# RWKV time mixing ahead of a SwiGLU FFN: both halves of mixing's products issued together, random trials on the start's schedule, the input flag made earlier

The chip is a Trainium2, one of its cores is used. The metric is the time of one execution in device microseconds (us), median of the runs; lower is better. The profiler's span of the same execution is some 1.7 to 1.8 us shorter than its time. Engine names in the profiles: PE is TensorE (PEld its weight loads), DVE VectorE, ACT ScalarE, POOL GpSimd, SP SyncE.

## The reference

```python
def _attn_ref(r, k, v, w, u):                 # B, H, S, D = 4, 8, 768, 48
    state = np.zeros((B, H, D, D)); y = np.zeros_like(r)
    for t in range(S):
        kt, vt, rt = (k[:, :, t], v[:, :, t], r[:, :, t])
        cur = np.einsum('bhd,bhe->bhde', u[None] * kt, vt)
        y[:, :, t] = np.einsum('bhd,bhde->bhe', rt, state + cur)
        state = w[None, :, :, None] * state + np.einsum('bhd,bhe->bhde', kt, vt)
    return y

def _moe_ref(x, w_gate, w_val, w_out, rms_g): # x: 3072 tokens x 384; d_ff 1536
    xn = x / np.sqrt(np.mean(x * x, axis=-1, keepdims=True) + 1e-06) * rms_g
    g = xn @ w_gate
    return (g / (1 + np.exp(-g)) * (xn @ w_val)) @ w_out
```

All in float32. The weights can arrive as 64-bit words, which the kernel rounds itself.

## The kernel before

The sequence is cut into 12 chunks of 64 steps. For a chunk, time mixing has four kinds of TensorE product, each for two halves of the batch: scores (`products`, 32 matmuls a half), outputs (`outputs`, 48), states (`states`, 32), and the sum of squares for the norm. The FFN then takes the chunk's 256 tokens. Chunks 0 and 1 and the mixing of 2 and 3 are the start, in which the weights are also loaded and rounded; from chunk 2 on, five blocks take two chunks each (the body, and the last block without mixing).

The start is ordered on the host by a list schedule. Every piece of work has an engine, a planned cost, its inputs, and for loads a planned landing time; the pieces are then issued in the order of their planned starts, and each engine works strictly in that order:

```python
    def run(self, cells, first, free, idle=None):
        goals, t = {}, first
        for i in cells:
            goals[i] = t
            t += self.ops[i][1]
        self.start = self.schedule(goals, free)
        ...                                       # cut: fillers for PE's clock
        for i in sorted(range(len(self.ops)), key=lambda i: (self.start[i], i)):
            ...
            self.ops[i][3]()                      # issue
    ...
    def loads(s):                                 # cost on SyncE, landing behind it
        add("SP", 2.6 if s == 0 else 2.0, [], ["CHr0", "CHr1", "CHk0", "CHk1"], lambda: load_chan(s), land=2)
    ...
        for half in range(2):                     # mixing in the start
            bank, key = next_at()                 # one of two PSUM banks
            add("PE", 0.97, [f"CHk{half}", f"MEr{half}", f"MOr{half}"], [key],
                lambda bank=bank, half=half: products(bank, half, CH[:, 1], ME, MO), name=f"A {s}")
            ...
```

The order of the body is written out: small letters are the first half, capitals the second (a scores, d diagonals, m masked copy, y outputs, u states; R and K decay r and k, 1 to 3 the bonus, h the state's k, r and n the norm):

```python
            plan = {
                (0, 2): "R", (1, 1): "K", (1, 4): "1", (2, 0): "2", (2, 2): "3d", (3, 0): "h", (3, 2): "aDm",
                (4, 0): "H", (4, 2): "AM", (4, 4): "y", (5, 2): "Y", (5, 4): "q", (5, 5): "u",
            }
        ...                                       # cut: six groups of seven FFN products
        mix(n, "U"), mix(n + 1, "R12")
        project(s, 0, False), mix(n, "r"), mix(n + 1, "3K")
        project(s, 0, True), mix(n + 1, "ad"), mix(n, "n")
        ...
```

48 checks read the weights once more (a load into one buffer, two ScalarE passes): 40 in four of the blocks and two behind each of the last four projections. Their sum becomes a flag; every engine loads it into a register and branches over a general path if it is 0.

## Time and profile before

674.57 us (674.41 to 676.01 over three runs; the profiled one took 675.09). Cut where the FFN's products, the blocks and the projections begin in the trace:

| stage | us |
|---|---|
| first FFN product begins | 27.35 |
| from there to the first block | 134.20 |
| four blocks with mixing | 105.56 + 102.97 + 102.97 + 101.07 = 412.57 |
| last block, to TensorE's last product | 85.82 |
| from there to the end | 13.36 |

TensorE is busy 96% of 673.3 us and VectorE 58%. TensorE's own rows do not say whether it could be faster.

### The profile page before, as it was taken

The numbers are of one execution on the slowest core, as the hardware profiler recorded it, in microseconds if no ns is written. First come the engines' busy times: TensorE is split into PE (matmuls) and PEld (weight loads), VectorE is DVE, ScalarE is ACT, GpSimd is POOL, SyncE is SP. The second block draws the span as 40 slices with busy tenths as digits, with TensorE's granted clock in tenths as the row PEclk, the third lists the DMA queues.
The fourth block names the chain that finished last, engine by engine and source line by source line (L and its number), as shares of the span: only waits on it lengthen the run. The fifth ranks groups of instructions, "written<-read, shape, count | busy, mean of one in ns | idle before, by whom it ended". The sixth has DMA issues, their size and how long they took to land.

```text
span 673.3 us, 15350 instructions
## 1 busy us (share of the span) xinstructions
PE 649.6 (96%) x6546; PEld 507.8 (75%) x6546; DVE 388.0 (58%) x560; ACT 342.5 (51%) x952; POOL 44.4 (7%) x39
## 2 busy tenths in 40 slices
PE   9969999999999999999999999999999999999992
PEld 8957777877878766888766888766888866888651
DVE  6998987345875724676644666652676553455200
ACT  5678470764262474474573574672564573433222
POOL 3434431000000000000000000000000000000000
PEclk9979999999999999999999999999999999999996
DMA  8997531262003141306341405332315221212141
GB/s 293 305 235 212 188 90 24 44 160 65 2 1 95 42 118 25 96 22 153 86 99 32 107 19 148 91 74 62 91 34 142 67 47 25 57 41 57 48 111 53
DMA packets 20079, 61.61 MB, mean 92 GB/s; under 512 B 3073, under 2 KB 6273, under 8 KB 18817
## 3 DMA queue, kind: packets, MB, share of 16 engines
q1 hardware_dynamic: 19696, 60.44, 33.8%
q8 instruction: 53, 0.87, 0.6%
q14 instruction: 26, 0.20, 0.1%
q10 hardware_dynamic: 304, 0.10, 0.1%
HBM read 55.81 MB, written 4.72 MB: 90 GB/s over the span
## 4 chain that ended last, share of the span: by engine, by line
PE 82%; DVE 8%; ACT 6%; DMA 2%; issue 2%; SPq 0%; DVEq 0%; ACTq 0%
PE po L90 24%; PE b L90 15%; PE a L90 10%; PE c L90 10%; PE first_c L90 4%; PE first_b L90 4%; PE py L90 4%; PE first_a L90 3%; PE at L90 3%; PE pa L90 3%; ACT MO L90 2%; PE pu L90 2%; DVE bits L90 2%; ACT ME L90 1%; DVE TOK L90 1%
## 5 line engine op out<-in xcount | busy, mean ns | idle before, releaser
L90 PE MATMUL po<-wo,h 128*128 128x384 f32 x480 | 162.5, 491 | 0.0
L90 PEld LDWEIGHTS po<-wo,h 128*128 128x128 f32 x480 | 89.2, 190 | 57.4 <-issue 0.3
L90 DVE TENSOR_TENSOR gv<-b,m 128x512 f32<-128x512 f32 x90 | 62.1, 690 | 66.3 <-PE b L90 65.6
L90 ACT ACTIVATE gv<-gv 128x512 f32<-128x512 f32 (+1 forms) x60 | 31.0, 518 | 49.6 <-DVE gv L90 49.6
L90 DVE TENSOR_TENSOR gv<-c,gv 128x512 f32<-128x512 f32 x60 | 41.4, 690 | 16.9 <-PE c L90 15.8
L90 ACT ACTIVATE ME<-dmask,du 64x64 f32<-64x64 f32 x176 | 43.8, 329 | 13.4 <-DVE du L90 13.0
L90 PE MATMUL a<-xa,wa 64*128 64x256 f32 x360 | 45.0, 382 | 1.9 <-DVE h L90 1.9
L90 PE MATMUL b<-xa,wa 64*128 64x256 f32 x360 | 45.3, 384 | 0.6 <-DVE gv L90 0.6
L90 ACT ACTIVATE MO<-dmask,du 64x64 f32<-64x64 f32 x176 | 44.4, 334 | 0.4
L90 PE MATMUL b<-t,wb 64*128 64x256 f32 x360 | 44.4, 379 | 0.0
L90 PE MATMUL c<-xb,s 64*128 64x256 f32 x360 | 44.3, 378 | 0.0
L90 PE MATMUL b<-t,s 64*128 64x256 f32 x360 | 44.0, 377 | 0.3 <-DVE gv L90 0.3
L90 PE MATMUL a<-xb,wb 64*128 64x256 f32 x360 | 43.9, 376 | 0.0
L90 PE MATMUL c<-t,s 64*128 64x256 f32 x360 | 43.9, 376 | 0.0
L90 PEld LDWEIGHTS a<-xa,wa 64*128 64x128 f32 x360 | 33.8, 187 | 8.8 <-DVE h L90 4.1
L90 PEld LDWEIGHTS b<-t,s 64*128 64x128 f32 x360 | 34.8, 187 | 4.7 <-DVE gv L90 0.7
L90 PEld LDWEIGHTS a<-xb,wb 64*128 64x128 f32 x360 | 34.8, 187 | 4.0
L90 PEld LDWEIGHTS c<-t,s 64*128 64x128 f32 x360 | 34.8, 187 | 4.0
L90 PEld LDWEIGHTS b<-t,wb 64*128 64x128 f32 x360 | 34.4, 187 | 4.4 <-DVE gv L90 0.3
L90 PEld LDWEIGHTS b<-xa,wa 64*128 64x128 f32 x360 | 33.4, 187 | 5.7 <-DVE gv L90 1.5
L90 PEld LDWEIGHTS c<-xb,s 64*128 64x128 f32 x360 | 34.5, 187 | 4.0
L90 ACT ACTIVATE gv<-a 128x256 f32<-128x256 f32 x30 | 11.4, 381 | 48.7 <-PE a L90 48.6
(146 smaller groups left out, 1100.7 us busy)
## 6 DMA issues: line engine op xcount, KB each, us to landing
TOK<-in_tok_dram SPq DMA_DIRECT2D x12, 768.0 KB, 4.9
chan<-in_chan_dram SPq DMA_DIRECT2D x22, 384.0 KB, 6.5
VS<-in_vpad_dram SPq DMA_DIRECT2D x24, 336.0 KB, 4.9
raw<-in_wot_dram SPq DMA_DIRECT2D x8, 576.0 KB, 5.7
again<-in_wka_dram SPq DMA_DIRECT2D x16, 288.0 KB, 2.8
out_dram<-o SPq DMA_DIRECT2D x48, 96.0 KB, 2.2
again<-in_wkb_dram SPq DMA_DIRECT2D x16, 288.0 KB, 2.9
again<-in_wot_dram SPq DMA_DIRECT2D x16, 288.0 KB, 2.8
```

What stands on the lines that cost most here:

```text
L90: return lambda *args, **kwargs: self.tc.keep_in_program_order(give(*args, **kwargs))
```

## The change

The intent: fewer changes between the forms of matmul on TensorE, a better order in the start, w, r and k ahead of u in the load queues, and the flag off the end of the program. Its core:

```diff
-    def run(self, cells, first, free, idle=None):
+    def run(self, cells, first, free, idle=None, trials=3000):
...
+        rng, best = random.Random(2), None
+        for trial in range(trials):
+            new = dict(goals)
+            if trial and rng.random() < 0.5:
+                a, by = rng.randrange(len(cells)), rng.uniform(-15, 15)
+                for i in cells[a : a + 1 + int(rng.expovariate(1 / 6))]:
+                    new[i] += by
+            elif trial:
+                new[rng.randrange(len(self.ops))] = rng.uniform(0, t)
+            start = self.schedule(new, free)
+            end = max(...) + 0.3 * sum(start[i] for i in cells) / len(cells)
+            if best is None or end <= best[0]:
+                best, goals = (end, start), new
...
-        add("SP", 2.6 if s == 0 else 2.0, [], ["CHr0", ...], lambda: load_chan(s), land=2)
+        add("SP", 2.3 if s == 0 else 1.8, [], ["CHr0", ...], lambda: load_chan(s), land=1.6)
...                      # in the start, from chunk 1 on: both halves one piece
+            add("PE", 2.35, score_keys[0] + score_keys[1], [two[0][1], two[1][1]],
+                lambda: [scores(0), scores(1)], name=f"A {s}")
...
-                (0, 2): "R", ..., (3, 2): "aDm",
-                (4, 0): "H", (4, 2): "AM", (4, 4): "y", (5, 2): "Y", (5, 4): "q", (5, 5): "u",
+                (0, 2): "R", ..., (3, 2): "D",
+                (3, 5): "aAm", (4, 1): "M", (4, 2): "H", (4, 4): "yY", (5, 3): "q",
...
+        mix(n, "uU"), mix(n + 1, "R123")
+        project(s, 0, False), mix(n, "r"), mix(n + 1, "KdD")
+        project(s, 0, True), mix(n + 1, "aA"), mix(n, "n")
+        project(s, 1, False), mix(n + 1, "mMh")
+        project(s, 1, True), mix(n + 1, "yYH")
...                      # checks: 6 now in the first block, 13 in the last; the load a turn ahead
-            for j in range(4):
-                project(s, j, False), project(s, j, True), check(), check()
...
+    project(s, 0, False), project(s, 0, True)
     pc = at_bank("pc")
-    nc.tensor.matmul(pc[0:1, 0:1], wrong, ones[:, 0:1], start=True, stop=True)
+    pe.matmul(pc[0:1, 0:1], wrong, ones[:, 0:1], start=True, stop=True)
+    n_bad = nc.values_load(bad[0:1, 0:1], min_val=0, max_val=1 << 20)
+    for j in range(1, 4):
+        project(s, j, False), project(s, j, True)
```

Planned costs of VectorE and ScalarE pieces also rise by 0.03 each, and other load times fall a little.

More of the change, by code (lines that the diff above doesn't have):

```diff
@@ L27 @@
+import random
 from collections import deque
@@ L107, in add @@
         n = len(self.ops)
+        if engine in ("DVE", "ACT"):
+            cost += 0.03
         self.ops.append((engine, cost, deps, give, land, port, name))
@@ L164, in run @@
             t += self.ops[i][1]
-        self.start = self.schedule(goals, free)
+        rng, best = random.Random(2), None
[8 more added lines that the diff above has]
+            start = self.schedule(new, free)
+            end = max(start[i] + self.ops[i][1] for i in cells) + 0.3 * sum(start[i] for i in cells) / len(cells)
+            if best is None or end <= best[0]:
+                best, goals = (end, start), new
+        self.start = best[1]
         busy = free["PE"]
@@ L209, in fast @@
     utab = c_tile([P, HP, D], "utab")
-    for z in range(2):
-        src = bass.AP(tensor=u_row.tensor, offset=u_row.offset + z * HP * D, ap=[[0, 64], [1, HP * D]])
-        act.dma_start(out=utab[64 - 64 * z : 128 - 64 * z].rearrange("p h d -> p (h d)"), in_=src)
     eps = c_tile([P, 1], "eps")
@@ L313, in load_v, with load_u @@
         sp.dma_start(out=VS[0:64, 1], in_=vpad[s, 0:64])
+    def load_u():
+        for z in range(2):
+            src = bass.AP(tensor=u_row.tensor, offset=u_row.offset + z * HP * D, ap=[[0, 64], [1, HP * D]])
+            sp.dma_start(out=utab[64 - 64 * z : 128 - 64 * z].rearrange("p h d -> p (h d)"), in_=src)
     wa = [c_tile([P, NQ, CC, P], f"wa_{i}") for i in range(WQ)]
@@ L340, in piece @@
         hi, lower = words[:, :, 1], words[:, :, 0].bitcast(U32)
-        p.add("SP", 1.6 * share, [], [r], lambda: sp.dma_start(out=raw, in_=part), land=2, name=f"load {n}")
+        p.add("SP", 1.35 * share, [], [r], lambda: sp.dma_start(out=raw, in_=part), land=1.8, name=f"load {n}")
         p.add(
@@ L588, in next_at @@
         return at[i], f"at{i}"
-    add("SP", 0.0, [], ["w"], lambda: None, land=2.8)
+    add("SP", 0.0, [], ["w"], lambda: None, land=2.4)
     add("DVE", 2.4, ["w"], ["pw"], powers, name="powers")
@@ L605, in loads @@
     def loads(s):
-        add("SP", 2.6 if s == 0 else 2.0, [], ["CHr0", "CHr1", "CHk0", "CHk1"], lambda: load_chan(s), land=2)
-        add("SP", 2.0, [], ["TOKr", "TOKk"], lambda: load_tok(s), land=2)
-        add("SP", 1.8, [], ["VSv"], lambda: load_v(s), land=2)
+        add("SP", 2.3 if s == 0 else 1.8, [], ["CHr0", "CHr1", "CHk0", "CHk1"], lambda: load_chan(s), land=1.6)
+        add("SP", 1.8, [], ["TOKr", "TOKk"], lambda: load_tok(s), land=1.8)
+        add("SP", 1.6, [], ["VSv"], lambda: load_v(s), land=1.8)
+        if s == 0:
+            add("SP", 0.5, [], ["utab"], load_u, land=1.8)
     def mixing(s):
@@ L616, in mixing @@
                 add(
-                    "PE", 0.97, ["ku", "CHr0", "CHr1"], [f"first{half}"],
+                    "PE", 1.05, ["ku", "CHr0", "CHr1"], [f"first{half}"],
                     lambda half=half: products(gv["a"][:, half], half, ku, CH[:, 0], CH[:, 0]), name=f"E {s}",
@@ L621, in mixing @@
             add("DVE", 0.95, ["TOKk"], ["TOKr"], lambda: bonus_1(s), port=True, name=f"bonus1 {s}")
-            add("DVE", 0.95, [], ["TOKr"], lambda: bonus_2(s), port=True, name=f"bonus2 {s}")
+            add("DVE", 0.95, ["utab"], ["TOKr"], lambda: bonus_2(s), port=True, name=f"bonus2 {s}")
             add("DVE", 0.94, ["TOKr"], ["du"], lambda: bonus_3(s), name=f"bonus3 {s}")
@@ L628, in mixing, with scores @@
             add(
-                "DVE", 0.05 + 0.585 * n, ["up"] + keys("CHr"), keys("MEr", "MEt"),
+                "DVE", 0.12 + 0.55 * n, ["up"] + keys("CHr"), keys("MEr", "MEt"),
                 lambda part=part: decay_r(s, *part), port=True, name=f"R {s}",
             )
-            add("ACT", 0.1 + 0.47 * n, keys("MEt"), keys("MOr"), lambda part=part: copy_r(s, *part), name=f"Rc {s}")
+            add("ACT", 0.16 + 0.44 * n, keys("MEt"), keys("MOr"), lambda part=part: copy_r(s, *part), name=f"Rc {s}")
             add(
-                "DVE", 0.05 + 0.585 * n, ["down"], keys("CHk"), lambda part=part: decay_k(s, *part), port=True,
+                "DVE", 0.12 + 0.55 * n, ["down"], keys("CHk"), lambda part=part: decay_k(s, *part), port=True,
                 name=f"K {s}",
             )
-        for half in range(2):
-            bank, key = next_at()
-            add(
-                "PE", 0.97, [f"CHk{half}", f"MEr{half}", f"MOr{half}"], [key],
-                lambda bank=bank, half=half: products(bank, half, CH[:, 1], ME, MO), name=f"A {s}",
-            )
+        two = [next_at() for _ in range(2)]
+        def scores(half):
+            products(two[half][0], half, CH[:, 1], ME, MO)
+        score_keys = [[f"CHk{half}", f"MEr{half}", f"MOr{half}"] for half in range(2)]
+        if quick:
+            for half in range(2):
+                add("PE", 1.05, score_keys[half], [two[half][1]], lambda half=half: scores(half), name=f"A {s}")
+        else:
+            add(
+                "PE", 2.35, score_keys[0] + score_keys[1], [two[0][1], two[1][1]], lambda: [scores(0), scores(1)],
+                name=f"A {s}",
+            )
+        for half in range(2):
+            bank, key = two[half]
             for side in range(2):
@@ L655, in mixing @@
                 )
+        pair = [next_at() for _ in range(2)]
+        output_keys = [[f"{x}{half}" for x in ("VSs", "MEr", "MOr", "MEt", "MOt")] for half in range(2)]
+        if quick:
+            for half in range(2):
+                add(
+                    "PE", 1.55, ["VSv"] + output_keys[half], [pair[half][1]],
+                    lambda half=half: outputs(pair[half][0], half), name=f"Y {s}",
+                )
+        else:
+            add(
+                "PE", 3.25, ["VSv"] + output_keys[0] + output_keys[1], [pair[0][1], pair[1][1]],
+                lambda: [outputs(pair[half][0], half) for half in range(2)], name=f"Y {s}",
+            )
         for half in range(2):
-            bank, key = next_at()
+            bank, key = pair[half]
             add(
-                "PE", 1.5, ["VSv"] + [f"{x}{half}" for x in ("VSs", "MEr", "MOr", "MEt", "MOt")], [key],
-                lambda bank=bank, half=half: outputs(bank, half), name=f"Y {s}",
-            )
-            add("ACT", 0.5, [key], [f"sq{half}"], lambda bank=bank, half=half: keep_squares(bank, half, sq), name=f"sq {s}")
-            add("ACT", 0.88, [key], [f"yT{half}"], lambda bank=bank, half=half: keep_outputs(bank, half, yT), name=f"yT {s}")
+                "ACT", 0.5, [key], [f"sq{half}"], lambda bank=bank, half=half: keep_squares(bank, half, sq),
+                name=f"sq {s}",
+            )
+            add(
+                "ACT", 0.88, [key], [f"yT{half}"], lambda bank=bank, half=half: keep_outputs(bank, half, yT),
+                name=f"yT {s}",
+            )
         bank, key = next_at()
@@ L680, in mixing @@
             add("DVE", 0.95, ["TOKk", "wk"], [f"KH{z}"], lambda z=z: state_k(s, z), port=True, name=f"h {s}")
-        for half in range(2):
-            bank, key = next_at()
-            add(
-                "PE", 0.97, ["KH0", "KH1", "khd", "VSv", f"VSs{half}"], [key],
-                lambda bank=bank, half=half: states(bank, half), name=f"U {s}",
-            )
+        last = [next_at() for _ in range(2)]
+        add(
+            "PE", 1.9, ["KH0", "KH1", "khd", "VSv", "VSs0", "VSs1"], [last[0][1], last[1][1]],
+            lambda: [states(last[half][0], half) for half in range(2)], name=f"U {s}",
+        )
+        for half in range(2):
+            bank, key = last[half]
             add("ACT", 1.07, [key], [f"VSs{half}"], lambda bank=bank, half=half: keep_states(bank, half), name=f"E {s}")
@@ L785, in warm @@
             pe.matmul(gv["c"][:, 0, 0:P], ones, ones, start=True, stop=True)
-    p.run(cells, 25.0, {"PE": 1.5, "DVE": 1.5, "ACT": 4.5, "POOL": 6.5, "SP": 1.2}, warm)
+    p.run(cells, 25.0, {"PE": 1.5, "DVE": 1.5, "ACT": 3.0, "POOL": 6.3, "SP": 1.7}, warm)
     def at_bank(name):
@@ L856, in fast @@
     again = deque(enumerate(parts))
+    staged = []
     def check():
-        if not again:
-            return
-        n, (src, k) = again.popleft()
-        raw = late["mine"].tile([P, CHECK], I64, name=f"again_{n}", tag="again")
-        nc.sync.dma_start(out=raw, in_=src[:, k * CHECK : (k + 1) * CHECK])
-        hi = raw.bitcast(I32).rearrange("p (n z) -> p n z", z=2)[:, :, 1].bitcast(FP32)
-        mag = late["mine"].tile([P, CHECK], FP32, name=f"mag_{n}", tag="mag")
-        act.activation(mag, hi, AF.Abs)
-        act.activation(mag, mag, AF.Relu, scale=-(2.0**15), bias=1.0, accum_out=seen[:, n : n + 1])
+        if staged:
+            n, raw = staged.pop()
+            hi = raw.bitcast(I32).rearrange("p (n z) -> p n z", z=2)[:, :, 1].bitcast(FP32)
+            mag = late["mine"].tile([P, CHECK], FP32, name=f"mag_{n}", tag="mag")
+            act.activation(mag, hi, AF.Abs)
+            act.activation(mag, mag, AF.Relu, scale=-(2.0**15), bias=1.0, accum_out=seen[:, n : n + 1])
+        if again:
+            n, (src, k) = again.popleft()
+            raw = late["mine"].tile([P, CHECK], I64, name=f"again_{n}", tag="again")
+            sp.dma_start(out=raw, in_=src[:, k * CHECK : (k + 1) * CHECK])
+            staged.append((n, raw))
     def group(s, m):
@@ L949, in fast @@
             plan = {
-                (0, 2): "R", (1, 1): "K", (1, 4): "1", (2, 0): "2", (2, 2): "3d", (3, 0): "h", (3, 2): "aDm",
-                (4, 0): "H", (4, 2): "AM", (4, 4): "y", (5, 2): "Y", (5, 4): "q", (5, 5): "u",
+                (0, 2): "R", (1, 1): "K", (1, 4): "1", (2, 0): "2", (2, 2): "3d", (3, 0): "h", (3, 2): "D",
+                (3, 5): "aAm", (4, 1): "M", (4, 2): "H", (4, 4): "yY", (5, 3): "q",
             }
@@ L954, in fast @@
             plan = {}
+        look = {(m, k) for m in range(NN // 2) for k in (2, 5) if m != 2}
+        if first_block:
+            look = {(m, k) for m, k in look if k == 5 or m == 4}
+        elif n == NS:
+            look |= {(2, 2), (2, 5), (5, 6)}
         for m in range(NN // 2):
@@ L962, in fast @@
                     mix(n, plan[m, k])
-                if not first_block and k in (2, 5) and m != 2:
+                if (m, k) in look:
                     check()
         if n == NS:
-            for j in range(4):
-                project(s, j, False), project(s, j, True), check(), check()
             break
-        mix(n, "U"), mix(n + 1, "R12")
-        project(s, 0, False), mix(n, "r"), mix(n + 1, "3K")
-        project(s, 0, True), mix(n + 1, "ad"), mix(n, "n")
-        project(s, 1, False), mix(n + 1, "ADmh")
@@ L973, in fast @@
-        project(s, 1, True), mix(n + 1, "yMH")
-        project(s, 2, False), mix(n + 1, "Yq")
+        mix(n, "uU"), mix(n + 1, "R123")
[3 more added lines that the diff above has]
+        project(s, 1, True), mix(n + 1, "yYH")
+        project(s, 2, False), mix(n + 1, "q")
         project(s, 2, True), mix(n + 1, "r")
-        project(s, 3, False), mix(n + 1, "un")
-        project(s, 3, True), mix(n + 1, "U")
+        project(s, 3, False), mix(n + 1, "n")
@@ L978, in fast @@
+        project(s, 3, True), mix(n + 1, "uU")
         for x in (1, 2, 3, 4):
             token_sum(n, x)
-    assert not again
+    assert not again and not staged
     tiny = c_tile(list(seen.shape), "tiny")
     if wide:
-        nc.vector.tensor_single_scalar(out=tiny, in_=seen, scalar=0.0, op=ALU.is_gt)
+        dve.tensor_single_scalar(out=tiny, in_=seen, scalar=0.0, op=ALU.is_gt)
     else:
-        nc.vector.memset(tiny, 0.0)
-    nc.vector.tensor_reduce(out=count[:, 1:2], in_=tiny, op=ALU.add, axis=AX.X)
+        dve.memset(tiny, 0.0)
@@ L989, in fast @@
+    dve.tensor_reduce(out=count[:, 1:2], in_=tiny, op=ALU.add, axis=AX.X)
     wrong = c_tile([P, 1], "wrong")
-    nc.vector.scalar_tensor_tensor(
+    dve.scalar_tensor_tensor(
         out=wrong, in0=count[:, 1:2], scalar=float(HP), in1=count[:, 0:1], op0=ALU.add, op1=ALU.subtract
     )
+    project(s, 0, False), project(s, 0, True)
     pc = at_bank("pc")
-    nc.tensor.matmul(pc[0:1, 0:1], wrong, ones[:, 0:1], start=True, stop=True)
-    nc.vector.tensor_copy(bad, pc[0:1, 0:1])
+    pe.matmul(pc[0:1, 0:1], wrong, ones[:, 0:1], start=True, stop=True)
@@ L998, in general @@
+    dve.tensor_copy(bad, pc[0:1, 0:1])
+    n_bad = nc.values_load(bad[0:1, 0:1], min_val=0, max_val=1 << 20)
+    for j in range(1, 4):
+        project(s, j, False), project(s, j, True)
+    return n_bad
 @with_exitstack
@@ L1404, in program @@
     chan, tok, vpad, wka, wkb, wot, cols, u_row, chan_0 = fast_args
-    fast(tc, chan, tok, vpad, wka, wkb, wot, cols, u_row, chan_0, out, bad)
-    n_bad = nc.values_load(bad[0:1, 0:1], min_val=0, max_val=1 << 20)
+    n_bad = fast(tc, chan, tok, vpad, wka, wkb, wot, cols, u_row, chan_0, out, bad)
     with tc.If(n_bad > 0):
```

## The prediction

> **What bounds the kernel now.** First the page's slices (tenths busy in 40 slices of 16.8 us):
>
> ```profile
> PE   9969999999999999999999999999999999999992
> DVE  6998987345875724676644666652676553455200
> PEclk9979999999999999999999999999999999999996
> ```
>
> TensorE (PE) is full from the fourth slice to the last but one; there are two holes, in the third slice, with a lowered clock, and at the end. VectorE (DVE) is the fuller engine only in the first 64 us. Then the busy time by stretch, cut where the stages change (stretch, its length, busy PE, weight loads, DVE, ACT, POOL, clock, DMA share, GB/s):
>
> ```profile
> 27.35:64.40 37.05, 31.44 (x364) 25.75 (x364) 33.38 (x42) 28.93 (x70) 17.59 (x12) 0.91 0.89 257
> 370.15:473.05 102.90, 102.71 (x1053) 79.40 (x1053) 58.78 (x83) 56.45 (x164) 0.00 (x0) 1.00 0.33 82
> 574.12:659.95 85.83, 85.82 (x601) 66.87 (x600) 29.41 (x49) 29.92 (x77) 0.00 (x0) 1.00 0.24 65
> 660.00:673.30 13.30, 0.19 (x2) 0.09 (x2) 0.70 (x4) 2.36 (x7) 0.00 (x0) 0.57 0.17 44
> ```
>
> So there are four regimes: a start bound by the chain to the first weights and by DVE; a body (five blocks of two chunks) in which PE alone sets the time; the last block, PE alone without time mixing; and 13.3 us in which PE has nothing to do. In the body the question is what PE's time is made of. The chain of waits there is PE from end to end (start, length, group):
>
> ```profile
> 401.99 1.08 PE pa L90 x32
> 403.07 1.50 PE b L90 x12
> 404.56 1.29 PE a L90 x12
> ...
> 437.70 3.87 PE po L90 x12
> 441.57 1.08 PE pa L90 x32
> 442.65 4.07 PE po L90 x12
> ```
>
> A product of 12 matmuls takes 1.29, but 1.50 behind a visit to time mixing (pa, py, pu); 12 projection matmuls take 3.87, but 4.07 behind one. Each visit costs 0.2 beyond its own time. Where the same chain has both halves together:
>
> ```profile
> 145.06 2.89 PE at L90 x96
> 147.94 1.50 PE first_c L90 x12
> ```
>
> 96 outputs matmuls in one visit take 2.89, against 2 x 1.52 for two visits of 48 (the row py x48 of the same view): 0.15 less. In the start, the timeline has 64 score matmuls from 12.83 to 14.84, 2.01 against 2 x 1.08: again 0.15. So one visit less saves 0.15 + 0.21 = **0.36 us**.
>
> Third, the hole in the start (timeline, then chain):
>
> ```profile
> 34.98 1.46 PE L90 MATMUL first_c<-xb,wb 64*128 64x256 f32 x12
> 41.80 0.37 PE L90 MATMUL at<-ME,chan 48*64 48x64 f32 x1 [5.35 <-DVE chan L90]
> ```
>
> ```profile
> 41.80 3.75 PE at L90 x64
> ```
>
> PE waits 5.35 us for chunk 1's decayed k. Afterwards the same 64 matmuls take 3.68 to the next start instead of 2.01, and the next 12 product matmuls 2.41 instead of 1.29: 1.7 + 1.1 = 2.8 more. The hole costs about 8.1 in all.
>
> Fourth, the end (timeline):
>
> ```profile
> 661.68 0.54 SPq L864 DMA_DIRECT2D again<-in_wot_dram  x1
> 664.79 0.46 ACT L90 ACTIVATE mag<-again 128x288 f32<-128x288 f32 x1 [3.39 <-DMA again<-in_wot_dram]
> 665.85 0.19 DVE L985 TENSOR_SCALAR tiny<-seen 128x48 f32<-128x48 f32 x1 [35.27 <-ACT mag L90]
> 666.75 0.15 DVE L995 CAST bad<-pc 1x1 int32<-1x1 f32 x1 [0.28 <-PE pc L994]
> ```
>
> The last product ends at 659.95 and the last store is issued at 660.48 to 661.6. Then comes one more weight check behind a DMA wait, the sum of the flags, its matmul and cast (to 666.9). The trace then has five register loads of the flag (to 667.5), the branch over the general path, and semaphores to 673.3.
>
> **What the Trainium skill says.** "TensorEngine Tiling (Array Packing)", Key Properties, says that changing the tiling mode drains TensorE; mixing's 48x64 and the FFN's 64x128 and 128x128 matmuls are different modes, and the trace agrees with 0.1 before and 0.1 after each change. "TensorE: Matmul & The Clock Gate", Part 1, puts the return to half clock at an idle window of about 3.4 us; the 5.35 us wait with the doubled durations behind it agrees, at a granted clock of 0.91 over that stretch. "Runtime: NRT & Kernel Launch", Instruction fetch mechanics, says that a taken branch to a page outside the window stalls on a fetch; the trace has 4.48 us of branch on PE, and 3.6 us from SyncE's branch (667.48) to its next instruction (671.06), so it agrees. "DMA: Bandwidth & Descriptors" gives some 2 us of fixed cost to a transfer; the page's median for the output store is 2.2.
>
> **The change, part by part.**
>
> *Halves together.* In a full block the PE order has 12 mixing visits, each of scores (pa), outputs (py), states (pu), for two chunks and two halves. The new plan has aA, yY and uU, so 6. Blocks 2, 4 and 6 lose 6 visits, block 8 loses 5 (chunk 11, the last, has no states): 23 x 0.36 = 8.3. In the scheduled start, outputs 1, states 0, states 1, scores 2 and states 2 stand apart in the trace, and scores 1 and 3, outputs 2 and 3 and states 3 already together: 5 x 0.36 = 1.8. The matmuls themselves stay the same, so nothing else of PE's time goes. All of it lies on the path, since PE is the path.
>
> *Random trials.* 3000 trials of a hill climb on the order of the start; no instruction more or less on the chip. What it can win is the 8.1 of the hole and delays ahead of the first product at 27.35. There DVE has non-urgent instructions in the way: the 2.63 us product for KH holds the reciprocal back by about 1, two weight conversions hold the first xa back by about 1.3 (26.11, where its bank was filled by 24.8). The first projection (3.87 us) is also held out of the hole only because its three gating DVE products of 0.42 stand at 42.8 to 46, not at 37. Against it, DVE is busy 33.4 of 37 us there, so moving one thing forward moves another back, and the trials optimise modelled times, not the chip's. I choose half of the hole: **4.0**.
>
> *w, r, k first.* The two loads of u leave ScalarE's queue and go behind the first loads of SyncE. Their packets began at 4.93, when those of w (to 5.6) and r, k (to 5.6) were nearly through, and ScalarE waited until 6.45 anyway. I give this 0 on its own.
>
> *Checks and flag.* 48 checks as before, now with the load issued one turn ahead: ScalarE loses the 26.6 us of DMA waits (9.9 + 9.6 + 7.1 in the waits), none of them on the path. All 48 are done before the last projections; the flag is made behind the first of four (7.74 us each, half of the two-chunk output). There PE must wait for its own matmul, the cast and its register load: from 666.52 to the end of the load at 667.43 in the old tail, with a switch, **+1.0**. At the end, the copy and store stay (to 661.6 for a PE end of 659.95); then SyncE's branch, 3.6, gives 665.2, and from there 2.2 as before (671.06 to 673.3): PE end + 7.45 instead of + 13.35, **-5.9**. PE's branch, 4.5 after its end, and the store's landing, 2.2 after its issue, are both shorter than that.
>
> *New waits.* Both mixing banks are now taken at once, and four masked copies (4 x 0.73) fall between scores and outputs. In the block there are 6 steps of 1.3 = 7.8 us between them; the second two copies stand behind the addition that follows the third step, so they end near 3 x 1.3 + 0.7 + 2 x 0.73 = 6.1, a margin of 1.7. Between projections there are 7.8 us too. Diagonals take 4 x 2.0 us of ScalarE, now issued earlier. I allow 1.0 over all blocks.
>
> Sum: 674.6 - 8.3 - 1.8 - 4.0 + 1.0 - 5.9 + 1.0 = **656.6**.
>
> **Rivals.**
>
> *The start does not move, or gets worse.* For it: DVE's 33.4 of 37 us, a model without the clock's fall after a wait, and paired scores and outputs in the start, which are harder to place. Against: the filler (the projection) is there, and the new costs (0.03 more per DVE and ACT instruction, DMA times nearer to the measured ones) make the model truer. Then 660.6; with 3 us lost, 663.6. The other way, with the whole hole gone and the first product 2 us earlier, 650.5.
>
> *DVE or the two banks become the bound in the block.* For it: the masked copies and the state product are bunched into little more than one group of 7 products (9.1 us), in which DVE already has 5.0: (62.1 + 41.4)/30 for the additions of the page's rows and 0.69 + 2 x 0.42 for h. Against: DVE is busy 58.8 of 102.9 over the block and PE waits for it 0.2 there. If each of four blocks waited 1 us more, 660.
>
> *The end does not shorten.* For it: the branch is taken later than the flag is read, so its fetch still follows the last instruction; PE could also lose more than 1.0 at the flag. Against: the 7 us from 659.95 to 666.9 contain nothing that needs the last product. At worst half of the 4.9 remains: 659.
>
> **Range and chances.** The body's 8.3 and the end's 4.9 are nearly counted (together +-2); the start is the wide term (+-4). The 2% line is 661.1; it takes both a start without gain and another step short to stay above it. I give 0.83 to faster, 0.16 to within 2%, 0.01 to slower; range 651 to 662.
>
> **What would show it right or wrong.** Right: scores x64 near 2.0, outputs x96 near 2.9, states x64 near 1.55 in the chain; blocks of about 100.9 us instead of 102.9; PE busy falling by about 10; the hole before chunk 1's scores under 3 us and no clock below 1 behind it; first steady block from about 156 instead of 161.55; a stop of about 1 us on PE between the first and second projection; 7.5 us from PE's end to the end. Wrong: PE waits on DVE gv or h or on masked copies inside the blocks, a new hole before 64 us, or more than 9 us after PE's end.

## The result, and the profile after

663.36 us (662.33 to 665.46 over four runs), against 674.99 of the kernel before in the same rounds: a ratio of 0.983, 95% interval 0.980 to 0.986. So it is faster by 1.7%, beyond the noise but not clear of 2%, and outside the predicted range. (Ratios are the mean time of one kernel's runs over that of the other's of the same rounds, so not quite the ratio of the medians quoted.)

The stages, from the traces (spans, so their sum is 1.7 to 1.8 below the times):

| stage, us | before | predicted | after | difference |
|---|---|---|---|---|
| first FFN product begins | 27.35 | | 35.28 | +7.93 |
| from there to the first block | 134.20 | | 126.96 | -7.24 |
| first block begins | 161.55 | 155.75 | 162.24 | +0.69 |
| four blocks | 412.57 | 405.3 | 406.58 | -5.99 |
| last block | 85.82 | 86.8 | 86.94 | +1.12 |
| tail | 13.36 | 7.45 | 6.39 | -6.97 |

The sum of the differences is -11.15, the spans' 673.3 and 662.2 differ by 11.1. Predicted was -18.0. Of the 6.9 that are missing, the start accounts for 6.5 (+0.7 where -5.8 was expected), the blocks for 1.3 more, and the tail gives 1.0 back. One trace is one run, and this one lies 0.6 above the median: four kernels below have the same start (e4_flag_end to e7_read_late), and in their traces the body begins at 160.0 to 160.9. So the start's shortfall is 4.3 to 6.5 us.

The body did what was expected. The chain of waits of the kernel after, around its third block (start, length, group):

```profile
404.23 2.01 PE pa L91 x64
406.24 1.50 PE c L91 x12
...
414.21 2.89 PE py L91 x96
...
440.91 7.94 PE po L91 x24
...
467.84 1.57 PE pu L91 x64
```

64 scores in 2.01, 96 outputs in 2.89, 64 states in 1.57, and 24 projection matmuls without a visit between them. A full block fell from 102.97 to 101.06.

The end too (timeline):

```profile
631.35 0.19 PE L91 MATMUL pc<-ones,wrong 128*1 128x1 f32 x2
631.58 0.14 DVE L91 CAST bad<-pc 1x1 int32<-1x1 f32 x1 [3.15 <-PE pc L91]
632.30 23.46 PE L91 MATMUL po<-wo,h 128*128 128x384 f32 x72 [0.77 <-DVE bad L91]
655.84 0.48 ACT L91 COPY o<-po 128x384 f32<-128x384 f32 x1 [7.26 <-PE po L91]
```

TensorE's flag matmul ends, the cast follows, and the next projection begins 0.95 after the flag's matmul began. After the last projection only a copy, a store and the branch are left.

The start did not. The page's slices of the kernel after:

```profile
PE   9699999999989999999999999999999999999996
DVE  5688688854876653576562577572566571555400
PEclk9898999999999999999999999999999999999999
```

The hole has moved from the third slice to the second, and the clock is lowered in the second and the fourth. The chain there:

```profile
14.98 10.68 DMA chan<-in_chan_dram
...
25.79 1.24 DVE ME L91
...
28.17 0.27 ACT ms L91
...
28.66 0.49 DVE diag L91 x2
29.15 0.14 issue
29.29 1.19 PE at L91 x2
```

Chunk 1's r and k are issued at 14.5 and 15.0, as soon as chunk 0's scores have read their buffer, and land at 24.1 and 25.7. VectorE's next instruction in order is the decay of chunk 1's r (ME), so it stands idle for 5.24 us; ScalarE's next is the copy of the decayed r, so chunk 0's square root (ms), whose sum was ready at about 22, is held to 28.17, and with it chunk 0's norm and the first FFN product.

The host's plan of this kernel, printed afterwards, says what the search believed:

```
   start    end   engine
   13.90   15.70  SP    load of chunk 1's r and k   (lands 1.6 + 0.2 later: 17.5)
   19.24   20.49  DVE   R 1
   20.69   21.76  ACT   Rc 1
   21.76   22.09  ACT   sqrt 0
   26.75   28.04  PE    g 0 0 0                     (first FFN product)
   plan's end: 153.9 us   (kernel before: 157.9; this code with one trial: 164.5)
```

With the load down at 17.5, R 1 in front of sqrt 0 costs nothing. On the chip it lands 8 us after the plan. (All times in this table are the plan's, not measured. R 1 is the decay of chunk 1's r, Rc 1 its copy, sqrt 0 chunk 0's square root.)

### The profile page after: what moved, and what is told of

Same layout as the page of the kernel before. It is cut to its first block, busy times and chain, and to the rows that moved or that the text cites. A ratio compares the mean times of both kernels' runs of the same rounds, so it can differ in the third digit from the quotient of the medians.

```text
span 662.2 us, 15313 instructions
## 1 busy us (share of the span) xinstructions
PE 640.5 (97%) x6534; PEld 506.8 (77%) x6534; DVE 385.9 (58%) x560; ACT 341.0 (52%) x952; POOL 44.6 (7%) x39
## 4 chain that ended last, share of the span: by engine, by line
PE 84%; ACT 6%; DVE 4%; DMA 3%; issue 2%; POOL 0%; SPq 0%; DVEq 0%; ACTq 0%; POOLq 0%
PE po L91 24%; PE b L91 15%; PE a L91 10%; PE c L91 9%; PE first_b L91 5%; PE first_c L91 4%; PE first_a L91 4%; PE at L91 4%; PE py L91 3%; PE pa L91 2%; PE pu L91 2%; DMA chan<-in_chan_dram 2%; ACT MO L91 2%; ACT ME L91 1%; DVE gv L91 1%
## 5 line engine op out<-in xcount | busy, mean ns | idle before, releaser
L91 PE MATMUL po<-wo,h 128*128 128x384 f32 x480 | 159.8, 489 | 0.8 <-DVE bad L91 0.8
L91 ACT COPY o<-po 128x384 f32<-128x384 f32 x20 | 9.5, 474 | 77.4 <-PE po L91 39.3
L91 ACT ACTIVATE mag<-again 128x288 f32<-128x288 f32 x48 | 22.1, 461 | 35.9 <-DMA again<-in_wot_dram 14.6
```

The lines of the kernel that those rows point to most:

```text
L91: return lambda *args, **kwargs: self.tc.keep_in_program_order(give(*args, **kwargs))
```

## The experiments

Theory A: the start's missing 6 to 7 us are one mistake of order, three pieces of chunk 1 placed ahead of chunk 0's norm because the plan has their load 8 us too early. Rival B: the start is bound by VectorE's work and the loads, and any order only shifts the hole. Each kernel is the changed one with one edit, unless it says otherwise. Times are medians of four runs, with the ratio to the kernel before of the same rounds.

### e1_move: the three pieces behind chunk 0's norm

```diff
         self.start = best[1]
+        at = {o[6]: i for i, o in enumerate(self.ops)}
+        for name, other, k in (("R 1", "x 0", 1), ("K 1", "x 0", 2), ("Rc 1", "xb 0", 3)):
+            self.start[at[name]] = max(self.start[at[name]], self.start[at[other]] + 0.001 * k)
```

> The changed kernel with three instructions moved in the order of issue and nothing else: chunk 1's decay of r and of k go behind chunk 0's x on VectorE, and the copy of chunk 1's decayed r goes behind chunk 0's exchange on ScalarE. Theory A (the two engines stand still from 20.6 to 25.8 us because the search put chunk 1's decay ahead of chunk 0's norm, and the load it needs landed at 25.7 us where the plan had 17.5): the first product comes at 27 to 29 us instead of 35.3, the body begins near 157 instead of 162.2, the time is 657 to 659. Rival B (the start is bound by VectorE's work and the loads, so order only shifts the hole): the first product comes earlier, but new waits follow and the body still begins at 161 to 163; time 662 to 665.

Measured: 657.41 us (657.12 to 658.36), ratio 0.975 (0.973 to 0.977), faster. VectorE's timeline:

```profile
22.24 0.17 DVE L91 RECIPROCAL ms<-ms 128x2 f32<-128x2 f32 x1 [1.63 <-ACT ms L91]
23.83 0.95 DVE L91 TENSOR_TENSOR xa<-yT_first,at 128x768 f32<-128x768 f32 x1 [0.43 <-PE at L91]
25.55 1.23 DVE L91 TENSOR_TENSOR ME<-chan,up 128x1024 f32<-128x1024 f32 x1 [0.76 <-DMA chan<-in_chan_dram]
```

The load still lands at 25.45, but chunk 0's norm and xa are done when it does. The first product comes at 26.41, a little ahead of the 27 to 29 expected, and the first block at 155.73: 5.8 before the kernel before, which is what the prediction gave the start. Blocks and tail stay as they were (406.6, 86.95, 6.57). Theory A holds, B falls.

### e2_land: the plan is told the measured landing

```diff
-        add("SP", 2.3 if s == 0 else 1.8, ..., lambda: load_chan(s), land=1.6)
+        add("SP", 2.3 if s == 0 else 1.8, ..., lambda: load_chan(s), land=9.4 if s == 1 else 1.6)
```

> The changed kernel with one number of the plan changed: chunk 1's load of r and k is planned to land 9.4 us after its issue slot instead of 1.6, as measured; the 3000 trials run again with it, and the plan's own end is 154.3 instead of 153.9. Theory A: the search now keeps chunk 1's decay behind chunk 0's norm; first product near 28, body from about 157, time 657 to 659. Rival B: as changed, 662 to 665.

Measured: 659.59 us (658.75 to 661.5), ratio 0.978 (0.976 to 0.981); the first product at 30.02, the body from 158.00. The search now leaves chunk 1's decay behind the norm on its own, with the same trials and seed. It is 2 us short of e1_move: its order is another one, in which TensorE waits for chunk 1's squares behind diagonals and roundings on ScalarE (total us, times, longest):

```profile
PE at L91 <- ACT sq_first L91: 2.2, 1, 2.2
```

Its granted clock is also 0.83 over 20 to 30 us and 0.89 over 50 to 60, where e1_move has 1.00. How the 2 us divide among these was not taken apart. A truer number mends most of the loss.

### e3_trials1: no search

```diff
-    def run(self, cells, first, free, idle=None, trials=3000):
+    def run(self, cells, first, free, idle=None, trials=1):
```

> The changed kernel with one trial instead of 3000, so the list schedule with its first goals, and all else as changed. Its plan ends at 164.5 against 153.9 with trials and 157.9 of the kernel before. If the trials bring what they plan apart from the late load: the body begins 6 to 10 us later than 162.2, time 668 to 674. Rival (the trials only moved the hole and bring nothing): time within 2 us of the changed kernel, 661 to 665.

Measured: 663.75 us (662.31 to 663.85), ratio 0.983 (0.981 to 0.985): the changed kernel's own time. The first product comes at 26.76, but then TensorE waits in another place:

```profile
PE first_a L91 <- DVE hbuf L91: 6.7, 1, 6.7
```

This is the longest of TensorE's waits there (total us, times, longest): the old hole, at VectorE's products for h. The body begins at 162.33, against 160.0 to 162.2 in the five traces with the searched order. So 10.6 planned us of search became 0 to 2 on the chip: the search closed this hole, and opened one about as large where its load time was wrong. With the order mended (e1_move) the search is worth 162.33 - 155.73 = 6.6 us in the start. Here my expectation was wrong; the rival was right in its number.

### e4_flag_end: the flag made behind the last projection again

```diff
-    project(s, 0, False), project(s, 0, True)
+    for j in range(4):
+        project(s, j, False), project(s, j, True)
     pc = at_bank("pc")
...
-    for j in range(1, 4):
-        project(s, j, False), project(s, j, True)
```

> The changed kernel with the flag's matmul, cast and register load behind the last projection instead of behind the first; the checks stay early. My prediction's step (the flag ahead of the end is worth 5.9 - 1.0): if the flag's place is what counts, 4 to 5 us slower, 667 to 668. New theory C (the 7 us of the old tail were the last checks and their loads, and those are gone either way; flag at the end costs about 0.9 us of matmul, cast and hand-over, flag ahead costs 1.1 us of stopped PE): within 0.7 us of the changed kernel, 662.5 to 664.

Measured: 662.71 us (662.47 to 662.87), ratio 0.982 (0.981 to 0.984): level with the changed kernel. Its trace has the last block at 85.82 again (1.12 less) and the tail at 7.50 (1.11 more). The place of the flag is worth nothing as it was done; the tail's 6 us come from the checks, which no longer stand between the last projection and the flag. The prediction had one sum for both.

### e5_apart: the body's halves apart again

```diff
-                (0, 2): "R", ..., (3, 2): "D",
-                (3, 5): "aAm", (4, 1): "M", (4, 2): "H", (4, 4): "yY", (5, 3): "q",
+                (0, 2): "R", ..., (3, 2): "aDm",
+                (4, 0): "H", (4, 2): "AM", (4, 4): "y", (5, 2): "Y", (5, 4): "q", (5, 5): "u",
```

and the seven lines of mixing among the projections as in the kernel before.

> The changed kernel with the order of the body's mixing put back to that of before (halves apart, 12 visits of TensorE a block and 11 in the last with mixing), start, checks and end as changed. My prediction's step: 0.36 us a visit, 23 visits, 8.3 us; from the traces of before and after the four blocks differ by 0.57 + 1.91 + 1.91 + 1.60 = 6.0. If the visits are the cause: blocks of 102.9 to 103 and 101.1 again, time 6 to 8 us above the changed kernel (669 to 671), PE's work otherwise the same. Rival (the shorter blocks come from the checks' loads being issued a turn ahead, which frees ScalarE of waits): the blocks stay near 101.1 and the time at 663.

Measured: 669.20 us (668.28 to 670.11), ratio 0.991 (0.989 to 0.993). Blocks of 106.20, 102.97, 102.97 and 101.06, so 6.6 us more than 406.58. The chain shows the visits again (start, length, group):

```profile
338.45 1.08 PE pa L91 x32
339.53 4.07 PE po L91 x12
343.59 1.08 PE pa L91 x32
344.67 4.07 PE po L91 x12
```

6.23 us for 64 scores and the projection between them, and 4.07 for the next, so 10.30; in the changed kernel it is 2.01 + 7.94 = 9.95 for the same. In the full blocks a visit less is worth 1.91 / 6 = 0.32 us. The checks' earlier loads give the body nothing.

### e6_looks: the first block's six checks moved to the last block

```diff
-            look = {(m, k) for m, k in look if k == 5 or m == 4}
+            look = set()
...
-            look |= {(2, 2), (2, 5), (5, 6)}
+            look |= {(2, 2), (2, 5), (5, 6)} | {(m, 0) for m in range(NN // 2)}
```

> The changed kernel with the six checks of the first block moved to the last block. Theory (a check of 1.1 us on ScalarE ahead of a Silu holds back VectorE and so TensorE's bank in the third group of the first block, the place where that block lost the 1.6 us it should have gained): the first block falls from 105.0 to 103.4 to 104, the last stays at 86.9 to 87.2; time 1 us less. Rival (the waits there are VectorE's extra sums, as before): the first block stays within 0.3 of 105.0.

Measured: 666.80 us (665.83 to 669.0), ratio 0.988 (0.986 to 0.990), slower than the changed kernel. The first block fell only to 104.56; the last rose from 86.94 to 91.50. The waits of the last block, up to its projections (total us, times, longest):

```profile
DVE h L91 <- ACT gv L91: 17.9, 11, 2.4
...
ACT mag L91 <- DMA again<-in_wot_dram: 9.4, 6, 2.4
ACT mag L91 <- DMA again<-in_wkb_dram: 7.5, 5, 3.2
ACT mag L91 <- DMA again<-in_wka_dram: 6.5, 4, 2.3
```

With checks every two or three products the load issued a turn ahead has not landed when its turn comes, ScalarE waits in order, its Silu comes late, and VectorE and TensorE with it. The first block of the changed kernel gained 0.57, 1.3 less than the 1.91 of the full blocks; moving its checks gives 0.4 of that back. e5_apart shows it from the other side: with the halves apart but the checks in, its first block is 106.20, 0.64 above the kernel before, so gathering is worth 106.20 - 104.99 = 1.21 there. TensorE's waits for VectorE's h and gv in this block go along: 2.2 us before, 2.6 in e5_apart, 3.2 in the changed kernel, 2.7 in e6_looks. So the checks cost 0.4 to 0.6, and gathering itself brings some 0.6 of new waits. Whether VectorE's extra sums in this block cause these was not tested. The theory's 103.4 to 104 was missed, and the rival's 0.3 slightly exceeded; the rival was nearer.

### e7_read_late: the flag's register loads one projection later

```diff
+    project(s, 1, False), project(s, 1, True)
     n_bad = nc.values_load(bad[0:1, 0:1], min_val=0, max_val=1 << 20)
-    for j in range(1, 4):
+    for j in range(2, 4):
```

> The changed kernel with the register loads of the flag one projection later than its matmul and cast. Theory: TensorE's stop of 1.1 us at the flag is its own register load waiting for the cast it fed; with 7.8 us of projection between, the last block falls from 86.94 to 85.9 to 86.2, the tail stays at 6.4; time 1 us less. Rival: the stop is the load itself and remains (86.9).

Measured: 662.43 us (661.42 to 664.77), ratio 0.982 (0.980 to 0.984), not to be told from the changed kernel by time, since the start scatters by more. In the trace the last block is 86.14 instead of 86.94, and the chain shows why:

```profile
629.78 0.12 PE pc L91 x2
629.90 23.43 PE po L91 x72
```

TensorE's stop of 0.95 was matmul, cast and its own register load in a row (the load's record is 0.49 of it, 631.76 to 632.25). Moved one projection later, the load no longer shows in the chain and TensorE goes straight on.

### e8_all, e9_best: the repairs together

e8_all is e1_move with the edits of e6_looks and e7_read_late.

> e1_move with both small repairs (no checks in the first block, register loads one projection later). If the three add up: 657.4 - 1.2 - 0.9, so 655 to 656, below both kernels; body from about 155.7, first block 103.4 to 104, last 86.1, tail 6.5. If one of them only shifts a wait, 656.5 to 657.5.

Measured: 661.69 us (660.49 to 662.03), ratio 0.980 (0.978 to 0.982): 4.3 above e1_move. Its last block is 90.68, the loss of e6_looks. e9_best instead moves a single check within the first block:

```diff
-            look = {(m, k) for m, k in look if k == 5 or m == 4}
+            look = {(0, 5), (3, 5), (4, 2), (4, 5), (5, 2), (5, 5)}
```

> e1_move with the flag's register loads one projection later, and the first block's check of its second group moved to its sixth group (not to the last block, where e6_looks and e8_all lost 3.8 to 4.6 us). If the gains add: last block 86.1 (-0.8), first block 104.5 (-0.5), start as e1_move (body from 155.7); time 656 to 656.8 against 657.4 of e1_move, below both kernels.

Measured: 657.90 us, ratio 0.974 (0.971 to 0.977), in two pairs: 656.11 and 656.62, 659.18 and 659.75. First block 104.55 and last block 86.13, as expected, but the profiled run is one of the slower pair and its body begins at 158.61. The issue order of the start is that of e1_move; but ScalarE stood 1.30 us for GpSimd's rounding, and TensorE then waited 1.6 us for chunk 1's squares where e1_move waited 0.4. Behind it the granted clock was lower (stretch, length, busy PE, weight loads, DVE, ACT, POOL, clock, DMA share, GB/s; e9_best, then e1_move):

```profile
50.00:60.00 10.00, 10.00 (x56) 7.00 (x56) 7.47 (x13) 5.97 (x9) 3.25 (x4) 0.82 0.52 173
50.00:60.00 10.00, 8.74 (x74) 7.14 (x74) 9.40 (x15) 6.74 (x9) 4.41 (x4) 1.00 0.67 224
```

From the start of the first projection to the next product it took 6.7 us instead of 5.4. The record has the clock of every run, and the two pairs differ in it: 0.997 and 0.999 over the whole execution in the quick pair, 0.992 and 0.990 in the slower one. But the wait alone does not decide it: e5_apart, e7_read_late and e10_behind have the same wait of 1.6 to 1.7 there and a clock of 1.00 over 40 to 60 us. What does was not tested. So runs of one and the same start scatter by some 3 us, the slower ones at the lower clock, and e9_best is inconclusive against e1_move by time.

### e10_behind: three weight loads behind chunk 1's load

```diff
         self.start = best[1]
+        where = {o[6]: i for i, o in enumerate(self.ops)}
+        for k in (3, 4, 5):
+            self.start[where[f"load {k}"]] = self.start[where["chan 1"]] + 0.001 * k
```

> The changed kernel with the weight loads 3, 4 and 5 issued behind chunk 1's load of r and k instead of ahead of it, and nothing else; their first use is at 34 us. Theory D (the load's 10.7 us are mostly a queue behind the six weight loads, whose packets run until 17.4): chunk 1's r and k land near 20 us, VectorE's stop of 5.2 us falls to under 1, the first product comes near 30, body from 157 to 158, time 657.5 to 659. Rival E (its own packets take the time: 96 of 8 KB, 0.5 to 0.9 us each from 17.4 to 25.7): it lands at 22 to 24, the first product at 32 to 33, time 660 to 661.5.

Measured: 658.70 us (658.4 to 658.8), ratio 0.976 (0.974 to 0.977), faster than before, with the order of VectorE and ScalarE left as the search made it. VectorE:

```profile
21.55 1.22 DVE L91 TENSOR_TENSOR ME<-chan,up 128x1024 f32<-128x1024 f32 x1 [1.63 <-PE at L91]
24.22 0.17 DVE L91 RECIPROCAL ms<-ms 128x2 f32<-128x2 f32 x1
```

Chunk 1's r and k land at 19.2 and 21.4, 4.9 and 4.2 earlier; the first product comes at 29.86, the body at 156.88. The page's idle note names TensorE as releaser of the decay, but the instruction starts 0.1 after the landing. So both D and E have a share: having three weight loads fewer ahead of it is worth 4.2 us, and the load's own packets still take 5.0 (15.4 to 20.4 in the packet records; 17.2 to 24.8 in the changed kernel, where the weights' packets run until 20.7 and not 17.4 as I expected). Its 8 KB packets, into 48 partitions, took 0.77 to 0.82 us (medians of 96 in four kernels), those of the first load, into 128 partitions, 0.31 (kernel before); why was not tested. Theory A is confirmed from the other side: when the load comes earlier, the same order costs 1.2 us against e1_move (body from 156.88, not 155.73).

### e11_best2: e9_best with e10_behind

> e9_best with weight loads 3, 4 and 5 behind chunk 1's load as in e10_behind. If an earlier landing helps beside the mended order too: chunk 1's decay at 24 instead of 25.5, first scores of chunk 1 earlier, time 0.5 to 1.5 us under e9_best (655 to 656). If the weights then come too late: level with e9_best or 1 us above.

Measured: 656.04 us (655.37 to 657.79), ratio 0.973 (0.971 to 0.975): the fastest kernel, 7.3 us under the changed one in medians. Against e9_best it is 1.9 lower in medians, but level with its quicker pair, so that the earlier load helps beside the mended order is not shown; chunk 1's decay does start at 24.59 instead of 25.5. Body from 155.29, blocks 104.57, 101.07, 101.06 and 99.49, last block 86.13, tail 6.41.

## Why the prediction was wrong

**What bounds it, and the visits: right, a little too large.** 0.36 a visit was read from pairs in the chain; in the full blocks it was 0.32 in the difference of whole blocks. In the first block the gain was 0.57 where 2.2 was due: 1.21 from gathering, less 0.64 for the checks that now stand there (e5_apart, e6_looks). "I allow 1.0 over all blocks" for new waits met the size by luck: the masked copies that it was meant for made no wait (the full block traced has the same 0.2 us of TensorE waits as before), and the 1.0 came in the first block, on h and gv, in part from the checks. Body: -6.0 against -8.3 + 1.0.

**Random trials: the failed step.** "I choose half of the hole: 4.0." With the 1.8 of the start's visits that made -5.8; measured was +0.7 (-1.5 to +0.7 over the five traces with this start). The old hole did go, as the stage from the first product to the body shows (-7.24). But a new one came ahead of the first product, 5.7 us long, and the lowered clock behind it (0.86 from 27 to 64 us). The prediction's own sign of being wrong, "a new hole before 64 us", is what came. The first rival had the right place ("the start does not move, or gets worse") and the figure of 660.6 to 663.6, but not the cause: none of its reasons is a late load, and VectorE's load, the first of them, is ruled out by e1_move, where VectorE does the same work. The cause is a late load: the plan has chunk 1's r and k landing 3.6 us after the start of their issue, the chip needs 11. e1_move shows it by order and e10_behind by the load.

This could have been read beforehand. In the trace of before the same load is issued at 15.0 and 15.4 and lands at 23.1 and 24.6, 8 to 9 us later, and its first reader starts at 34.63, so nothing waited. I looked at what VectorE waits for; I did not compare the plan's landing times, which the diff made shorter still, with the landings in the trace. I also wrote that the new costs "make the model truer", which was false for the one number that mattered.

"TensorE: Matmul & The Clock Gate" (table of the specification) calls the queues of ScalarE and VectorE strict FIFOs. The trace agrees: VectorE idles 5.24 us with the first weights' conversion behind the waiting decay, and starts that conversion at 28.07, directly behind it. Here a piece placed too early cost 5.24 us of VectorE and the 5.7 us hole on TensorE behind it.

**w, r, k first: forecast 0**, and no gain shows: w landed at 6.4 before and at 7.0 after (6.2 to 7.3 in the kernels of the experiments). It was not tested alone.

**Checks and flag: right in sum, wrong in its parts.** -5.9 + 1.0 was expected, -6.97 + 1.12 came. The tail is 1.0 shorter than my 7.45 because the branch and the semaphores behind it took less than in the old trace: SyncE's branch is followed by its next instruction after 2.7 us (657.51 to 660.23) instead of 3.6. But the flag's place, for which the prediction had no sum apart from the checks', is worth nothing as it was done (e4_flag_end); its stop is avoidable, and then it is worth 0.8 (e7_read_late). One reading was wrong: "ScalarE loses the 26.6 us of DMA waits". The checks' waits are 14.6 + 11.2 + 10.0 = 35.8 us in the trace after. The checks share one buffer, and already before the change a load was issued about 0.5 us behind the read of the check ahead of it (read at 273.00, next load at 273.50; after, 273.12 and 273.62), so "a turn ahead" changed little. In the full blocks these waits cost nothing, since TensorE sets the time there.

**The range.** 651 to 662 covers a start without gain (660.6) and 1.4 more, but not the rival's 663.6. The time lay 1.4 above its upper end because the body's shortfall of 1.3 came together with a start without gain and a little loss.

## What to carry to other kernels

Before trusting a host-made schedule, hold its assumed landing time of every load against the landing in the trace, also of loads that nobody waits for at present: a search can use the slack that a wrong number promises, and an engine that works in order then stands still (here 5.24 us, for a load 8 us later than planned). Products of another shape are best gathered: here each visit to another form of matmul cost 0.3 us, and the same instructions were issued. When a chain at the end is moved, ask which of its links made the time; a value read back by the engine that made it should be read a stage later.

## What the Trainium skill lacked or had wrong

- "TensorEngine Tiling (Array Packing)", Key Properties, has the drain at a change of tiling mode but no cost: the traces show 0.1 us before and 0.1 after a visit, and about 0.15 more for splitting a run of 64 or 96 small matmuls in two; 0.32 to 0.36 a visit in all.
- "DMA: Bandwidth & Descriptors" gives about 2 us fixed cost and a rate for a transfer alone (fitted on GpSimd's path); I found no figure for a load behind others. Here two loads of 384 KB took 10.7 us behind six weight loads and 6.5 with three of them moved behind (e10_behind).
- "TensorE: Matmul & The Clock Gate", Part 1, speaks of an idle window of about 3.4 us. Here the clock fell behind shorter waits too: behind 1.6 us ahead of chunk 1's squares in e9_best (0.84 and 0.82) and in the changed kernel (0.83 over 50 to 60 us), while the same wait in e5_apart, e7_read_late and e10_behind left it at 1.00. The wait is followed by 12 matmuls of one column; whether these count as idle was not tested.
- "Runtime: NRT & Kernel Launch", Instruction fetch mechanics, has the stall of a taken branch without a figure. Here the branch's record on TensorE is 3.6 to 4.5 us long over all traces, and SyncE's next instruction follows its branch after 2.7 to 3.6.
